# A hand-written order for an attention and phase-mixing kernel, replaced by another order of the same steps

## The chip, the cores and the metric

The kernel runs on one core of one Trainium2 chip. The metric is the device time of the whole program in microseconds (us), lower is better. A profile of one execution stands beside the times; its span runs from the first to the last instruction of the program on the core.

A core has five engines with an instruction stream each: PE (TensorE, matrix products and transposes by an identity matrix; PEld is its weight load, which overlaps), DVE (VectorE), ACT (ScalarE), POOL (GpSimd) and SP (SyncE, which here only issues DMAs). Results of PE land in PSUM, which this kernel uses as 8 banks of 512 float32 per partition.

## The reference

The inputs are `q`, `k`, `v` of 8 batches x 8 heads x 576 positions x 64, and four weight matrices. Two attentions are added: one over positions averaged in groups of four (144 of them), whose result is repeated four times, and one over a band of seven neighbours. Their sum is the input `x` (8 x 576 x 512) of a mixing step with a cosine and a sine of a learned phase.

```python
q_d = q.reshape(B, H, Sd, 4, D).mean(axis=3)          # k_d, v_d alike
out_up = np.repeat(sm_attn(q_d, k_d, v_d), 4, axis=2)
mask = np.abs(pos[:, None] - pos[None, :]) < 4
scores = np.where(mask, scale * q @ k.T, -1e9)
out_local = softmax(scores) @ v
x = (out_up + out_local)                              # heads side by side: 576 x 512
...
theta = x @ w_theta
y = w_tok_r @ (x * cos(theta)) + w_tok_i @ (x * sin(theta))
u = x + y
out = u + np.maximum(u @ w_ch, 0.0)
```

## The kernel before

Everything is unrolled. The work is cut into some 1,190 steps, and a table of words, `ORDER`, says in which order they are emitted. A word is a kind of two letters and a place: the PSUM bank or pair of banks that a PE step writes, the staging slot (0 to f) that a load fills, or the engine (`v` DVE, `a` ACT, `g` POOL) that does a cast, an eviction or a sum. `tp45` is a transpose into banks 4 and 5; `ckv` a cast of a piece of `k` on DVE; `lk8` a load of `k` into slot 8. The indices of a step (batch, piece) don't stand in the word: the n-th word of a kind is the n-th piece of that kind, in a fixed order. `pin()` ties each instruction to the one before it on its engine, so the order of the words is the order in each engine's queue. Between engines the tile framework puts the waits that data, banks and buffers need.

The steps of one batch, with the lines of the profile:

- Loads `lk`, `lq` (L287), `lv`/`lw` (L348) into 16 float32 staging slots; casts to bf16 `ck`, `cq` (L296) and `cv` (L396); transposes `tp` on PE (L303) and their copies `ev` (L316) into `kT`, `qT`. Batch 7 has its `k` and `q` transposed by DMA instead (`dk` L307, then `ev` L313). Batch 0 has its `v` loaded, cast and transposed in another way at the very start: `l1` L366, `c1` L372, `t1` L377, `e1` L380, `x1` L389, `cv` L394.
- Means of four: `kd`, `qd`, one reduction on DVE (L322) or two additions on POOL (L330 and L333 or L336); `pv` (L404, L407) and `vd` (L412, L415) for `v`.
- Coarse attention: scores `sd` (L426), exponential `ed` on ACT (L437), products `nd` (L447, L452), division `xn` on DVE (L457, L458), transpose `xd` (L466) and its copy `xc` (L470).
- Band attention: scores `ps` (L482) in three units of two, two and one chunks, exponential `ex` on ACT (L490), multiplication with the band `mk` on POOL or DVE (L501), products `po` (L511), division `nm` on DVE (L519, L520), transpose `xt` (L533), and `xa` on DVE (L541), which adds the coarse part and gives `xT`, the transposed `x`.
- Phase: `th` (L552) and `tt` (L564) on PE, cosine and sine `cs` (L557, L558) and `ct` (L569, L570) on ACT. `xm` transposes `xT` back on PE (L591) in batches 0 to 5; in 6 and 7 `dx` does it by DMA, four DMAs a batch (L601). `zz` on DVE (L616, or L611 with `dx`) multiplies. The last 64 positions go through `zt` (L573) and `zp`, `zc` (L583, L586) in batches 0 to 3, through a DMA `dz` (L577) in 4 to 7.
- Mixing: `mx`, eight groups of nine matmuls a batch (L632), and `ua` on DVE (L637), which gives `uT`; `up`, `uc` (L646, L649) on PE or `du` by DMA, four a batch (L641), bring `u` back.
- The end: `ch` (L662) on PE, `rl` on DVE (L667), the store `st` (L671). The last 64 positions of two batches together: `ut` (L652), `dt` by DMA (L686), `ht` on PE (L691), `rt` on DVE (L695), stores `ss`, `sr` (L700).

`wm` (L755) is a number of matmuls on a tile of zeros that nobody reads. `wm483` writes bank 4 with eight matmuls of 512 columns and one of 3 x 64. They stand at the start, where PE waits for loads, casts and copies. `te` and `ts` (L761) load the table of the exponential or of the sine into ACT ahead of its use.

A pair of banks is taken as any two banks:

```python
def pair(w):
    a, b = sorted(int(x) for x in w)
    return PS[:, a:b + 1:b - a, :]
```

All DMAs stand in the one queue of SP, in the order of the words. A DMA that has to wait there (for a slot, or for the result that it stores) holds back all DMAs behind it.

Of the kernel before, what the change touches and what calls it, by code (L numbers as in the profile page):

```python
# [58 lines left out]
lq9 x11 tp45 kcg cqa cva cqg x16 cqg lka cvv cvv lqb evv cvv ckg cva lkc kdg cka cqa lqd ckg lke laf wm772 tp23 evv  # L59
wm754 tp67 pv45 tp01 qdv kcg eva vdv la0 kdg lq1 eva cka wm256 ps23 ex ps67 lk2 qdv ps01 mkv wm446 sd45 sd23 ex ed  # L60
po67 ed cav cqg la3 po45 nm nm lk5 nd67 cqa xn mkg nd23 ex xn cag cka tp45 lq6 eva la4 po01 po67 lb8 nm lb9 xd2 wm303
tp45 lb7 cqa lba lqb ckg lbc lbe xcv mkg lbd lbf xt01 caa nm lb1 po23 kdg xa eva lv0 lv2 xt67 tp45 lw cag th0 lv5 cba
cbg lw cbg cqg lw xa xm1 nm th6 xt23 lv6 evv th7 ts cs xa zz tp45 cbg cbg wp0 cs wcv lv3 xm6 cs tt2 xm3 th7 wp1 lw xm0
zz zz lw qdv lk8 wcv eva ct lk4 lq9 cs cbg cbg cbg cbg wp6 wca wp3 wp2 wp4 wp5 wca wp1 wcv wcv wcv wp2 ztg ps67 ps45
qdg wcv te ex wcv ex lq7 kdg lkb lka zz lkc lqe lkd zp1 zcv cvv lqf mx3 cvg cvg cvg mkv ua cvg lq1 mx2 sd01 ps67 lv0
mkv lq2 ex po45 mx3 nm sd67 ua cqg po45 ed lw po01 nm ua nm mx2 ed ua pv67 po45 lq5 mx3 cqg vda nm nd01 ua cka up2
nd67 mkg cka xn ckg ckg lk6 uca xn up3 tp45 uca tp01 xd6 eva ckg xt23 mx7 xcv eva qdg xa xt45 po01 th6 cqg xa lv3 ckg
lv9 tp23 nm ts cs cqa th4 lq7 xm5 xt01 th6 evv cs tp23 xa zz cqa tt4 ua tp01 kdg cs ct cqg evv ztv th5 lw evv lw xm7
zz cs tp23 mx6 xm4 kdg zp5 qdg ua eva zz cvv ps01 cqa ps23 lv8 xm7 kdg zz zcv lk4 te ex lw mx6 mx4 ua mx5 sd01 mkv lvb
lw ua ex po67 mkv cva ps23 qdg lca lcc utg ed lce nm mx4 cvg ex lcd lvf ua lk1 po01 lk2 sd67 lw po23 ckg nm cqa nm mx5  # L70
ckg ed tp01 cvg ua lq5 eva tp67 mx4 lq0 cca ua up5 evv cvg ua ccg ccg pv23 mkg ucv vda lk3 qdv ps01 ps67 ex up4 mx5
ccv nd23 ex ua nd01 uca kdg ch5 po67 xn ps23 ckg cka lv9 mx4 xn tp01 lw ex mkg rl nm lk6 cva ckg xd5 sd23 ua cqg xcv
xt67 lv7 eva mx4 lw lv4 lw cvg xa lv8 lw ed xt01 po23 po67 th5 ua ch4 cqa ts cs xa nm nm th0 po23 lqb xt67 rl up1 cs
nm kdg th5 xm0 xa cs xm4 tp23 xm6 tt7 mkg cvg zz th0 lqc ucv zz st up1 cvg up5 ch4 eva ucv ckg ct ucv ch1 zz po23 cs
sd67 lve lva rl mkv te ed cvg pv45 lqd lk1 ztg cqg ch0 rl rl lk2 ch1 qdg nm lq3 vda tp67 nd45 rl cqa xm0 lqf eva lw zz
xn nd23 zp1 utg lw xn tp67 zca lk5 lq9 kdg mx0 up1 ua po45 lv0 eva ckg lk7 ps23 nm lw po67 nm ckg lv4 uca mx0 tp45 lk6
qdg mx1 ua xd0 ps67 ua lv8 ex eva xca ckg sd23 xt45 xa lw mx1 mkg st cvg ua ed mx0 ex mx1 mkv ua th0 po23 ua xt45 ts
cs xa xt67 mx1 xm0 xa th4 xm5 lqb zz ua tt0 kdg xm1 cvv ckg cvv th6 ch7 cqg cka cqg cs ct nm cs lvc cqg lk1 ztv tp23
eva lw th0 rl zz cs cqg zz tp67 evv cvg xm4 zz st zp5 zca ch1 rl cva tp23 mx0 po67 ua eva ps45 lw nm po23 lv2 te ex
lv5 mx1 pv67 lke cqg st mx0 po45 dt vda nm lk7 mkv st lqd po23 ckg ua ua qdg sd67 ch1 qdg nm nm ht0 cka ed rt lv3 up6  # L80
up7 cvg ucv uca nd45 kdg cqg nd23 mx0 xn lw xn ps67 ss ps45 ex ex xd2 mx3 tp67 xcv up2 cva ua uca tp45 lq6 rl evv up0
cqg lw eva ch1 ua lvf xt67 ps23 ucv sd45 xa cva st ex lw lq9 rl lk4 mx0 sd23 ed xt67 ua ckg xa lva qdg lw mkv kdv xt45
mx1 cvg th0 ua st lvb mx6 ua lw ed mkg tp23 ts cs utg lw mx7 cqg xa ua up6 po01 po45 cvg eva uca pv23 tt7 nm vda lq0
nm th6 xm0 zz nd45 ct cs ch1 lv1 xn cva st tp23 nd67 cva xn up0 th4 xm5 th6 zz sr eva xm7 xm5 ps23 lv8 lvc rl uca cs
po01 ch4 zz lw cs nm zz ztg ch7 te ex dz xd6 ch5 cvg rl lw lqe utg rl mkg po01 ps23 st mx4 lw lkd up7 cqg cka st ex
up2 uca nm ch3 rl xt01 kdg st st cvg xcv cva qdg ckg ua xa mkg uca po45 pv67 mx2 nm mx0 ua lk6 sd45 vda lk2 rl lq7
xt67 cqg ua ps23 xa mx1 lv5 ed po45 ua lq3 nm st mkv cqg dt ex dk9 sd23 xt67 ckg ed mx0 mkg du xa nd45 ch1 ckg ua po23
# [711 lines left out]
```

## Time and profile before

| | |
|---|---|
| three runs | 236.89, 238.10, 238.81 us; median 238.10 |
| span of the profiled execution | 232.1 us |
| outside the span, against the median | 6.0 us |
| PE busy | 220.7 us, 95% of the span |
| DVE, ACT, POOL busy | 191.8, 156.1, 135.5 us |
| DMA, read and written | 33.98 and 9.44 MB of HBM, mean 213 GB/s with the transfers inside SBUF |

The page gives no device time of its own for the profiled execution: its span is 232.1 us, and the 6.0 us to the median are what lies around a span. Matmuls are pipelined, and a row of PE counts each from its start to its modelled end, so that a PE that is busy is not a PE at its peak: what a group of matmuls costs the queue is read from how far apart many of them in a row start.

### The profile page before, as it was taken

Reading aid. Unit: us, or ns where it says so; the run is one execution under the profiler, and the core shown is the slowest. Engines: PE = TensorE matmul, PEld = TensorE weight load, DVE = VectorE, ACT = ScalarE, POOL = GpSimd, SP = SyncE. Lnnn points to the kernel's source line nnn. Section 1 sums busy time; section 2 is a strip of 40 time slices with the busy share of each in tenths; the row PEclk is TensorE's granted clock in tenths of the full one; section 3 lists DMA queues with packets and bytes.
Section 4 is the critical chain, followed back from the end, with each engine's and each line's share of the span. In section 5 each row is a group of like instructions: output and inputs, shape, how many; then the busy total and the mean of one; then the engine's idle time right before and its main releaser. Section 6 shows DMA issues by size and latency. Waiting matters only on the chain.

```text
span 232.1 us, 9462 instructions
## 1 busy us (share of the span) xinstructions
PE 220.7 (95%) x3986; PEld 153.2 (66%) x3986; DVE 191.8 (83%) x365; ACT 156.1 (67%) x241; POOL 135.5 (58%) x179
## 2 busy tenths in 40 slices
PE   7998899999998999999999999999999998999991
PEld 2665678777776765776768766676676563767750
DVE  6699999989997988868997997799889967567572
ACT  3359999799877989867976979857766591620000
POOL 7468989869999656897472837767386510000000
PEclk9999999999999999999999999999999999999998
DMA  6999989999999899989606895899957766556676
GB/s 204 382 392 390 298 134 252 365 263 193 264 263 195 224 290 208 203 209 210 174 3 178 226 234 147 293 249 173 153 122 189 144 138 100 154 126 182 138 235 217
DMA packets 76795, 49.41 MB, mean 213 GB/s; under 512 B 61136, under 2 KB 61392, under 8 KB 76752
## 3 DMA queue, kind: packets, MB, share of 16 engines
q1 hardware_dynamic: 76752, 48.81, 84.6%
q8 instruction: 31, 0.51, 1.1%
q14 instruction: 12, 0.10, 0.2%
HBM read 33.98 MB, written 9.44 MB: 187 GB/s over the span
## 4 chain that ended last, share of the span: by engine, by line
PE 72%; DVE 12%; DMA 5%; SPq 3%; issue 3%; ACT 2%; DVEq 0%
PE PS L632 24%; PE PS L662 10%; PE PS L552 9%; PE PS L303 5%; PE PS L755 4%; PE PS L511 3%; DVE xT L541 3%; DMA out_dram<-osb 2%; DVE pm L501 2%; PE PS L591 2%; PE PS L482 2%; DMA st<-xT 2%; SPq L641 2%; PE PS L533 2%; DVE uT L637 2%
## 5 line engine op out<-in xcount | busy, mean ns | idle before, releaser
L632 PE MATMUL PS<-WT,z 128*128 128x288 bf16 x576 | 77.9, 286 | 1.7 <-issue 1.7
L632 PEld LDWEIGHTS <-z 128*128 128x128 bf16 x576 | 53.8, 98 | 17.5 <-issue 2.8
L637 DVE TENSOR_TENSOR uT<-PS,xT 128x288 bf16<-128x288 f32 x64 | 28.1, 450 | 11.4 <-PE PS L632 11.1
L552 PE MATMUL PS<-wth,xT 128*128 128x512 bf16 x128 | 32.3, 380 | 0.7 <-DVE xT L541 0.7
L557 ACT ACTIVATE cs<-PS,pihc 128x512 bf16<-128x512 f32 x32 | 22.3, 696 | 15.1 <-PE PS L552 9.9
L662 PE MATMUL PS<-wch,uT 128*128 128x512 bf16 (+1 forms) x132 | 30.6, 373 | 0.0
L520 DVE TENSOR_TENSOR tmp<-PS,rl 128x512 bf16<-128x512 f32 x40 | 27.7, 692 | 1.4
L541 DVE TENSOR_TENSOR xT<-PS,xdT 128x928 bf16<-128x928 f32 (+1 forms) x24 | 22.7, 952 | 3.4 <-PE PS L533 3.1
L490 ACT ACTIVATE pm<-PS 128x1024 bf16<-128x1024 f32 (+1 forms) x24 | 20.4, 877 | 7.0 <-PE PS L482 2.7
L501 POOL TENSOR_TENSOR pm<-pm,band 128x1024 bf16<-128x1024 bf16 (+1 forms) x13 | 22.2, 1709 | 2.9 <-ACT pm L490 2.9
L667 DVE SCALAR_TENSOR_TENSOR osb<-PS,ur 128x512 f32<-128x512 f32 (+1 forms) x33 | 21.8, 669 | 2.4 <-PE PS L662 1.6
L330 POOL TENSOR_TENSOR two<-kT 128x580 f32<-128x580 bf16 x15 | 17.5, 1163 | 6.1 <-ACT kT L316 5.2
L296 POOL CAST q_tm<-st 128x576 bf16<-128x576 f32 x22 | 14.4, 664 | 10.8 <-DMA st<-in_q_dram 10.8
L662 PEld LDWEIGHTS <-uT 128*128 128x128 bf16 x132 | 12.2, 98 | 12.2 <-issue 0.3
L558 ACT ACTIVATE cs<-PS 128x512 bf16<-128x512 f32 x32 | 19.4, 605 | 0.0
L330 POOL TENSOR_TENSOR two<-qT 128x576 f32<-128x576 bf16 x11 | 12.8, 1167 | 10.5 <-ACT qT L316 7.1
L552 PEld LDWEIGHTS <-xT 128*128 128x128 bf16 x128 | 11.2, 98 | 10.7 <-issue 1.3
L616 DVE TENSOR_TENSOR z<-PS,cs 128x1024 bf16<-128x1024 bf16 x24 | 16.2, 685 | 1.9 <-PE PS L591 0.9
L437 ACT ACTIVATE pd<-PS 128x864 bf16<-128x864 f32 x16 | 14.1, 889 | 5.2 <-PE PS L426 5.2
L761 ACT ACT_TABLE_LOAD x13 | 16.7, 1283 | 0.2
L296 POOL CAST k_tm<-st 128x576 bf16<-128x576 f32 x21 | 14.4, 695 | 1.4 <-DMA st<-in_k_dram 1.4
L396 POOL CAST v_w<-st 128x512 bf16<-128x512 f32 x21 | 13.3, 653 | 1.3 <-DMA st<-in_v_dram 1.2
(119 smaller groups left out, 419.3 us busy)
## 6 DMA issues: line engine op xcount, KB each, us to landing
st<-in_q_dram SPq DMA_DIRECT2D x32, 288.0 KB, 6.3
st<-in_k_dram SPq DMA_DIRECT2D x32, 288.0 KB, 6.0
st<-in_v_dram SPq DMA_DIRECT2D x70, 128.0 KB, 4.7
out_dram<-osb SPq DMA_DIRECT2D x31, 256.0 KB, 2.9
out_dram<-osb SPq DMA_DIRECT2D x10, 128.0 KB, 2.4
st<-in_v_dram SPq DMA_DIRECT2D x4, 288.0 KB, 3.7
st<-in_moe_w_tok_r_dram SPq DMA_DIRECT2D x4, 288.0 KB, 6.2
st<-in_moe_w_tok_i_dram SPq DMA_DIRECT2D x4, 288.0 KB, 7.2
```

Source lines behind the costliest of these rows:

```text
L296: COPY[w](out=to[:, r, :], in_=of[:, r, :])
L330: nc.gpsimd.tensor_tensor(out=t, in0=src[:, :, 0:2], in1=src[:, :, 2:4], op=ALU.add)
L490: nc.scalar.activation(out=pm[(3 * b + u) % NPM][:, :, 0:n].rearrange("p e c j w -> p e (c j w)"), in_=at.pop(("ps", b, u))[:, :, 0:4 * W ...
L501: EW[w].tensor_tensor(out=t, in0=t, in1=m, op=ALU.mult)
L520: nc.vector.tensor_tensor(out=tmp[(NCH * b + c) % NTMP].rearrange("p g (j d) -> p g j d", d=D), in0=ps[:, :, :, 0:D], in1=r.unsqueeze(3).t ...
L541: nc.vector.tensor_tensor(out=xT[b % 2][:, :, lo:lo + cnt].rearrange("p e (m j) -> p e m j", j=4), in0=at.pop(("xt", b, u))[:, :, 0:cnt].r ...
L552: nc.tensor.matmul(out=ps, lhsT=xT[b % 2][:, dc, P * c:P * c + P], rhs=wth[:, dc, :], start=(dc == 0), stop=(dc == 3))
L557: nc.scalar.activation(out=t[:, 0, :], in_=ps, func=AF.Sin, bias=pihc, scale=1.0)
L632: nc.tensor.matmul(out=ps, lhsT=z[b % 2][:, j, P * dc:P * dc + P], rhs=WT[:, j, cols], start=(j == 0), stop=(j == 8))
L637: nc.vector.tensor_tensor(out=uT[b % 2][:, dc, cols], in0=at.pop(("mx", b, i)), in1=xT[b % 2][:, dc, cols], op=ALU.add)
L662: nc.tensor.matmul(out=ps[:, cols], lhsT=uT[b % 2][:, dc, P * c:P * c + P], rhs=wch[:, dc, cols], start=(dc == 0), stop=(dc == 3))
L667: nc.vector.scalar_tensor_tensor(out=o[:, cols], in0=at["ch", b, c][:, cols], scalar=0.0, in1=ur[b % 2][:, c, cols], op0=ALU.max, op1=ALU.add)
```

## The change

Only the table `ORDER` changes: all its 39 lines are new. The steps, their indices, tiles, buffers and shapes stay. In the new table

- the steps stand in another order, on every engine and in SP's queue;
- banks, slots and engines are other ones. The pairs of banks were 01, 23, 45 and 67 (150 results, and 8 `pv`, whose two banks were such pairs too); now they are 01, 23, 45, 67 and also 12, 34 and 56 (20 of 150). `pv` has two results of one bank each and now also takes 07, 57 and 04;
- `wm` has 22 matmuls of 512 columns and 25 x 64 columns; before 40 and 31 x 64. They still stand at the start only;
- casts and evictions have moved between engines. Counts before and now: `ck` on DVE 1 and 11, on POOL 21 and 12, on ACT 10 and 9; `cq` on DVE 0 and 4, on ACT 10 and 7; `mk` on DVE 11 and 6, on POOL 13 and 18; `qd` on DVE 5 and 1, on POOL 11 and 15; `ev` on DVE 9 and 7; `te` and `ts` together 13 and 15.

```diff
 ORDER = """
-l10 l11 l12 c1v c1a c1g k0 l13 kcv wm061 t101 c1g lq4 e1v wm256 t123 lk5 lk6 kca e1v wm483 x12 x13 lk7 ckv lq8 x10 cka
...
+l10 l11 c1v c1v l12 c1g l13 c1g wm785 t101 wm712 t123 lk4 ckv lk5 ckg wm736 tp45 lk6 ckg lq7 e1a e1v x13 x12 x10 lq8
...
 """
```

(`k0` is a word without an instruction.)

Three places follow. First the queue of DVE at the start of the program, from behind the first casts of `v` to the first multiplication with the band (`z_103` holds `v` of batch 0 here, `xT_102` its transpose, `k_tm` and `q_tm` the cast `k` and `q`, `st` the staging slots). Before:

```order
L296 CAST k_tm_74<-st 128x8x64
L296 CAST k_tm_74<-st 128x64
L394 CAST v_w_70<-PS 128x8x64 x2
L316 COPY kT_62<-PS 128x2x576
L394 CAST v_w_70<-PS 128x8x64
L316 COPY qT_64<-PS 128x1152
L322 TENSOR_REDUCE qd_68<-qT_64 128x288
L412 CAST vd_72<-PS 128x8x64
L415 CAST vd_72<-PS 32x4x64 x2
L322 TENSOR_REDUCE qd_68<-qT_64 128x288
L501 TENSOR_TENSOR pm_83<-pm_83,band 128x1024
```

Now, without the rows between `q_tm_78` and `k_tm_76` (two more casts of `q`, `vd` and `kd`):

```order
L296 CAST k_tm_74<-st 128x8x64
L296 CAST k_tm_74<-st 128x64
L380 COPY xT_102<-PS 128x1152
L231 COPY pu_132<-full_136 64x32 x2
L231 COPY pu_133<-full_137 64x32 x2
L231 COPY band<-full_135 64x64 x2
L394 CAST v_w_70<-PS 128x8x64
L296 CAST k_tm_75<-st 128x8x64
L296 CAST k_tm_75<-st 128x64
L394 CAST v_w_70<-PS 128x8x64
L296 CAST q_tm_78<-st 128x8x64
L296 CAST q_tm_78<-st 128x64
```

The copies of `kT` and `qT` (`ev`) and the sums of `qd` have left this stretch of DVE's queue for ACT and POOL; casts of `k` and `q` and small constants have come in, and the first cast of `k` now stands ahead of the copy of `xT_102`.

Second, the queue of DVE where batch 7's `xT` and batch 6's `z` are made (`xT_102` is batch 7 and `z_103` batch 6 here). Before:

```order
L470 COPY xdT_100<-PS 128x576
L541 TENSOR_TENSOR xT_102<-PS,xdT_100 128x4x232
L611 TENSOR_TENSOR z_103<-st,cs_105 128x1024
L541 TENSOR_TENSOR xT_102<-PS,xdT_100 128x4x232
L611 TENSOR_TENSOR z_103<-st,cs_106 128x1024
L541 TENSOR_TENSOR xT_102<-PS,xdT_100 128x4x112
L611 TENSOR_TENSOR z_103<-st,cs_107 128x1024
L611 TENSOR_TENSOR z_103<-st,cs_108 128x1024
```

Now, a little further down, where `uT_111` is batch 6 and `z_104` batch 7:

```order
L637 TENSOR_TENSOR uT_111<-PS,xT_101 128x288
L695 SCALAR_TENSOR_TENSOR osb_119<-PS,utr 128x512
L611 TENSOR_TENSOR z_104<-st,cs_105 128x1024
L611 TENSOR_TENSOR z_104<-st,cs_106 128x1024
L611 TENSOR_TENSOR z_104<-st,cs_107 128x1024
L637 TENSOR_TENSOR uT_111<-PS,xT_101 128x288
```

All three `xa` of batch 7 now stand ahead of the four `zz` of batch 6; and three `zz` of batch 7 stand between the first and the second `ua` of batch 6.

Third, the queue of SP that feeds those `zz`: `st_126<-xT0_101` are the `dx` of batch 6, `st_126<-xT1_102` those of batch 7. Now:

```order
L601 DMA_TRANSPOSE st_126<-xT0_101 128x4x128
L671 DMA out_0_dram<-osb0_118 128x512
L671 DMA out_0_dram<-osb1_119 128x512
L671 DMA out_0_dram<-osb3_121 128x512
L671 DMA out_0_dram<-osb4_122 128x512
L700 DMA out_0_dram<-osb2_120 64x512
L641 DMA_TRANSPOSE ur1_114<-uT1_112 128x4x128 x3
L601 DMA_TRANSPOSE st_126<-xT0_101 128x4x128 x3
L577 DMA_TRANSPOSE z0_103<-zT_110 128x4x128
L641 DMA_TRANSPOSE ur1_114<-uT1_112 128x4x128
L671 DMA out_0_dram<-osb0_118 128x512
L601 DMA_TRANSPOSE st_126<-xT1_102 128x4x128 x3
```

Behind these come `dt`, `dz`, one store and the fourth `dx` of batch 7. Before, two `dx` of batch 6 stood first, with two stores, three `du`, two `dx`, a store, `dz`, `dt`, a `du`, two `dx`, two stores and two `dx` behind them: 14 transposes and 5 stores from the first `dx` to the last, now 15 and 7.

More of the change, by code (lines that the diff above doesn't have):

```diff
@@ L57 @@
 ORDER = """
-l10 l11 l12 c1v c1a c1g k0 l13 kcv wm061 t101 c1g lq4 e1v wm256 t123 lk5 lk6 kca e1v wm483 x12 x13 lk7 ckv lq8 x10 cka
[L59 to L87, printed above, removed]
@@ new lines @@
+eva kcv kcv kcg kcv cvv x11 cva lk9 lqa lqb x17 ckv lk0 lk2 lk3 cva cvv cva cqg cqg cqv wm623 tp23 eva tp45 eva pv07
+cqv wm621 tp12 vdv eva kdg qdg qdg kdv wm652 ps01 ps23 la4 cag ckv lb5 cka ckv ex ex cbg lb6 cbg mkv wm716 tp67 la7
+lk8 mkg sd01 sd45 ed lq9 lqa ed po23 nm po01 caa lqb cqg eva nd23 cqa cqg nm nd45 ps01 la1 lac ex mkg xn cka xn po67
+po23 cag xd4 kdg lb2 lv0 lb3 lb4 tp01 xca nm nm xt67 lv5 tp45 xa xt23 cbg cbg lq7 eva xa cbg caa ts po01 nm xm6 lb6
+lbd th7 th3 lb9 xt01 cbg cbg cbg lbb evv cs th2 xa xm7 zz cqg wp4 lq8 cs cs zz xm5 tt3 zz th0 ct lva wp7 wp6 cs wcv
@@ L97 @@
+mx1 mx4 ua ztg dz st rt mx5 mx7 dx ss zz zz cs zz ua du mx1 cs zz mx3 mx0 ua ua rl rl ua mx2 mx7 mx6 ua ua mx1 mx3 ua
+ua mx2 mx0 ua ua ua ua sr mx1 ch3 st ua du du utv du ua ua du du st ch0 st rl st du ch1 ch2 ch3 ch7 ch6 ch5 du uta rl
+st rl rl st dt rl st st st rl st rl rm st su rl st ht7 rt sr ss k0
 """
```

39 lines of the change are left out of this document (30 added, 9 removed).

## The prediction

> **What bounds the kernel now.** I read the page's span and busy times first, then the busy time of each engine in a few stretches, then the chain of waits at its end. The page:
>
> ```profile
> span 232.1 us, 9462 instructions
> PE 220.7 (95%) x3986; PEld 153.2 (66%) x3986; DVE 191.8 (83%) x365; ACT 156.1 (67%) x241; POOL 135.5 (58%) x179
> ```
>
> PE is busy for all but 11.4 us. The stretches show where those are; columns: from and to, length, then busy us (and instructions) of PE, PEld, DVE, ACT and POOL, the granted clock, the DMA share and GB/s:
>
> ```profile
> 6.00:18.00 12.00, 12.00 (x136) 7.32 (x133) 9.82 (x12) 5.41 (x8) 7.04 (x13) 1.00 1.04 390
> 18.00:30.00 12.00, 10.26 (x333) 7.34 (x334) 11.44 (x23) 11.95 (x18) 10.90 (x14) 1.00 1.05 325
> 40.00:180.00 140.00, 137.42 (x2810) 99.15 (x2802) 122.33 (x223) 112.76 (x171) 100.82 (x118) 1.00 0.91 210
> 196.00:227.10 31.10, 31.04 (x224) 20.62 (x222) 21.09 (x43) 5.23 (x10) 0.00 (x0) 1.00 0.64 170
> ```
>
> From 40 to 180 us PE idles for 2.6 of 140 us, DVE for 17.7; from 196 us to PE's end, 0.06 of 31.1. So the body is PE's own queue, with DVE next. From 18 to 30 us DVE (11.44 of 12) and ACT (11.95) are full and PE is not: there PE waits. From 6 to 18 us PE looks full, but much of that is `wm`:
>
> ```profile
> L755 PE MATMUL PS<-warm 128*128 128x512 bf16 (+5 forms) x48 | 11.6, 380 | 0.0
> ```
>
> These 11.6 us stand where PE would wait. What an order can win is then 11.6 us of fill, 1.7 us between 18 and 30 us, and some 3 us behind. The useful work of PE doesn't change: the same groups stand in both tables. Its pace at the end:
>
> ```profile
> 204.93 14.33 PE PS L632 x117
> 219.26 6.92 PE PS L662 x36
> ```
>
> 117 matmuls are 13 `mx` groups, 1.10 us each; the 36 of `ch` are 7 whole groups and one in halves, 0.87 us each.
>
> **The start.** The first `th` needs `xa`, and `xa` comes at the end of a long queue on DVE. The timeline at its two ends (start, length, engine, line, what; in brackets the idle time ahead and what ended it):
>
> ```profile
> 7.08 0.67 POOL L372 CAST z<-st 128x576 bf16<-128x576 f32 x1 [0.18 <-DMA st<-in_v_dram]
> 8.51 1.36 DVE L380 COPY xT<-PS 128x1152 bf16<-128x1152 bf16 x1 [0.56 <-PE PS L377]
> 9.24 0.67 ACT L296 CAST k_tm<-st 128x576 bf16<-128x576 f32 x1 [3.92 <-DMA st<-in_k_dram]
> 27.75 1.11 DVE L541 TENSOR_TENSOR xT<-PS,xdT 128x928 bf16<-128x928 f32 x1
> 27.89 1.04 PE L552 MATMUL PS<-wth,xT 128*128 128x512 bf16 x4
> ```
>
> From 9.87 us (the copy's end) to 28.86 us (the second `xa`'s) DVE hardly waits, so what leaves this stretch of its queue brings `th` forward. The prices, by form:
>
> ```profile
> L296 DVE CAST k_tm<-st 128x512 bf16<-128x512 f32 x1 | 0.4, 427 | 0.0
> L372 DVE CAST z<-st 128x64 bf16<-128x64 f32 x1 | 0.3, 285 | 0.0
> L231 DVE COPY pu<-full 64x32 bf16<-64x32 bf16 x2 | 0.4, 207 | 0.0
> L322 DVE TENSOR_REDUCE qd<-qT 128x288 bf16<-128x1152 bf16 x5 | 6.7, 1346 | 0.1
> L316 DVE COPY kT<-PS 128x1152 bf16<-128x1152 bf16 x6 | 8.1, 1352 | 0.3 <-PE PS L303 0.3
> L394 DVE CAST v_w<-PS 128x512 bf16<-128x512 f32 x3 | 2.0, 685 | 0.5 <-PE PS L389 0.5
> L243 DVE CAST wth<-st 128x512 bf16<-128x512 f32 x1 | 0.4, 420 | 0.0
> ```
>
> In come five casts of `k` and `q` (0.43 + 0.29 each, 3.6 us), six small copies (1.2) and one sum of `kd` (taken as 1.35, as `qd`): 6.1 us. Out go two `ev` (2.7), two `qd` (2.7), one cast of `v_w` (0.7), one of `wth` (0.4), the copy `xc` to ACT (taken as 0.4) and the first cast of `k`, which now lies ahead of the copy (0.7): 7.6 us. That is 1.5 us less. The stretch starts later, though: the copy now stands behind the first cast of `k`. The fourth load of `v` landed at 7.08 us, the sixth load (`k`) at 9.24; the first `k` is now the fifth, so at 8.2, cast by 8.9, and the copy ends at 10.2 rather than 9.87. Together -1.2 us. Behind this comes POOL's first `mk`, which now has two sums of `qd` and three weight casts ahead of it, and ends about when it did (23 us). The ends: nothing, if the first `k` lands at 9.24 as it did; and -5.0, if PE's waits shrink as their fill does: 40 x 512 + 31 x 64 = 22,464 columns took 11.6 us, 22 x 512 + 25 x 64 = 12,864 would take 6.6. I take -1.2, because DVE's queue is the row that was full.
>
> **The body.** The casts that moved, and what they cost beside POOL's work:
>
> ```profile
> L396 DVE CAST v_w<-st x5: 410/793/1266, 38.0 to 173.6; 128x512 bf16<-128x512 f32 x5
> 40.14 0.72 DVE L501 TENSOR_TENSOR pm<-pm,band 128x1024 bf16<-128x1024 bf16 x1
> 177.35 2.19 DVE L501 TENSOR_TENSOR pm<-pm,band 128x1024 bf16<-128x1024 bf16 x1
> 176.87 3.69 POOL L501 TENSOR_TENSOR pm<-pm,band 128x1024 bf16<-128x1024 bf16 x2 [1.93 <-ACT pm L490]
> L501 DVE TENSOR_TENSOR pm<-pm,band 128x1024 bf16<-128x1024 bf16 x9 | 11.0, 1217 | 0.0
> L501 POOL TENSOR_TENSOR pm<-pm,band 128x1024 bf16<-128x1024 bf16 x7 | 14.9, 2123 | 2.9 <-ACT pm L490 2.9
> L330 POOL TENSOR_TENSOR two<-qT 128x576 f32<-128x576 bf16 x11 | 12.8, 1167 | 10.5 <-ACT qT L316 7.1 <-ACT qT L313 1.8 <-PE PS L533 1.4
> L336 POOL TENSOR_TENSOR qd<-two 128x288 bf16<-128x288 f32 x11 | 7.6, 695 | 0.9
> L296 POOL CAST k_tm<-st 128x576 bf16<-128x576 f32 x21 | 14.4, 695 | 1.4 <-DMA st<-in_k_dram 1.4
> ```
>
> Over the whole program DVE gives up four `qd` (5.4 us), four long `mk` and a short one (5.5), two `ev` and the copy of batch 0 (4.1), and takes 14 casts (14 x 0.71 = 9.9); the small moves add some 2: about -3 us. POOL takes four long `mk` (8.5), four `qd` (4 x 1.86 = 7.4) and gives up nine casts of `k` (6.3): with the small moves +13 of 135.5. ACT loads a table twice more and drops casts: about even. DVE's saving lies at the start; ahead of the first two `mx` groups it has 4.7 us less to do at these means, so behind them some 1.7 us more. It had 17.7 us to spare from 40 to 180 us, and PE paid 2.6 us. I take +0.8 us for tighter turns of banks and DVE's later work; the ends are -2.6 (all of PE's idle time goes) and +4.5 (below).
>
> The row of 2.19 us: the same multiplication took 0.72 us at 40.14, and 2.19 where POOL did one of its own from 176.87 on. DVE's ended 0.5 us after POOL's first. So DVE waited for POOL. The Trainium skill, "SBUF — State Buffer", section "Who interferes with whom", says that DVE and GpSimd share a pair of ports as an exclusive lock: a DVE instruction with two SBUF inputs, or a copy or cast in a 2-port mode, waits for a whole GpSimd instruction that came first, or makes it wait. The trace agrees (2.19 against 0.72). By this rule each of the 14 casts on DVE would wait up to one POOL multiplication, and the move of `mk` to POOL would lengthen what they wait for; that speaks against the change.
>
> **The end.** Before, a `zz` of batch 6 that waited for a DMA stood ahead of `xa` of batch 7, and PE waited for that `xa`:
>
> ```profile
> 195.82 1.02 PE L552 MATMUL PS<-wth,xT 128*128 128x512 bf16 x4 [0.66 <-DVE xT L541]
> 205.58 0.68 DVE L611 TENSOR_TENSOR z<-st,cs 128x1024 bf16<-128x1024 bf16 x1
> 206.18 0.45 DVE L637 TENSOR_TENSOR uT<-PS,xT 128x288 bf16<-128x288 f32 x1
> ```
>
> This 0.66 us goes, since `xa` is ahead now. What is late next is `zz` of batch 7: three of them stand ahead of the second `ua` of batch 6, whose bank (1) the sixth `mx` of batch 6 needs. A `zz` needs all four `dx` of its batch, and the fourth is the last of 15 transposes and 7 stores on SP. SP's prices:
>
> ```profile
> 180.10 2.53 SPq L601 DMA_TRANSPOSE st<-xT  x2
> 183.11 1.58 SPq L671 DMA_DIRECT2D out_dram<-osb  x2
> 184.78 3.84 SPq L641 DMA_TRANSPOSE ur<-uT  x3
> 201.58 2.52 SPq L601 DMA_TRANSPOSE st<-xT  x2
> ```
>
> A transpose holds SP for 1.27 us, a store for up to 0.79; 15 and 7 are at least 19 and up to 24.6 us; take 23. From the last issue's end (204.10) to the `zz` behind it (205.58) it was 1.5 us, then three `zz` at 0.6 and a `ua` of 0.45: 26.8 us after the first `dx` of batch 6 the bank is free. PE has, from that `dx`'s place in the table to the `mx`, 8 `mx` groups (8.8), 15 of `th`, `ch` and `ht` (13.0) and small groups (estimated 3): 24.8 us. So the `dx` has to issue 2 us before PE passes its place. Its data (`xa` of batch 6) are there some five PE groups ahead, and two `du` are the only transposes just before it, so I take it that it does, and price the end at -0.6; the ends are -0.7 and +3.5, where the `dx` comes 1.5 us behind its place instead.
>
> **The sum.** -1.2 + 0.8 - 0.6 = -1.0 us on the span of 232.1, so 231.1; with the 6.0 us around the span that separate it from the median of 238.1, **237.1 us**. The runs before lie within 0.8% of each other, so a difference of 1% (2.4 us) is about what can be told from none.
>
> **The rivals.**
>
> *The fill tells the truth* (faster): PE's waits at the start shrink by 5.0 us. 238.1 - 5.0 + 0.8 - 0.6 = 233.3. For it: the fill is cut at every place, and ACT, also full from 18 to 30 us, loses two casts there. Against: DVE's queue shrinks by only 1.2.
>
> *SP is late at the end* (slower): the `dx` of batch 6 issue at their place or later, the sixth `mx` of batch 6 waits for `ua` behind three `zz`. It decides once SP is more than 2 us later than I take it; at 1.5 us behind its place it costs 3.5: 237.1 + 3.5 = 240.6. For it: SP's row is nearly unbroken from 184 to 204 us, and the new stretch has three entries more. Against: the `xa` come earlier.
>
> *DVE waits for POOL* (slower): the casts at 0.8 us rather than 0.4 (the median of five against the least) and up to 1.3 add 14 x 0.4 = 5.6 to 12 us to DVE; six `mk` fewer take back 6 x 0.5 = 3.0. At +4.5 on PE's path, in place of the 0.8: 240.8. It decides once DVE's idle share in the body (17.7 of 140) falls under a tenth. This is what the Trainium skill's rule above would make of it.
>
> That the table isn't followed can't be, since each queue is pinned to it; that other pairs of banks cost or save something by themselves, no row shows.
>
> **The numbers.** The forecast has 0.38, and its own range is 235 to 239.3: of it 0.12 are below 235.7 (faster by over 1%), 0.25 within, 0.01 above 240.5. The fill: 0.25, all faster. SP late: 0.14, of which 0.10 slower, 0.04 within. DVE behind POOL: 0.17, 0.13 and 0.04. Gains and losses that cancel in other places: 0.06, within. Faster 0.37, same 0.39, slower 0.24. The range of 232.6 to 241.6 takes in all four times and leaves out what lies beyond the fill's and the two slow cases' own prices.
>
> **What would show it.** Right: the first `th` near 26.7 us, `wm` near 6.6 us, PE idle 2 to 4 us from 40 to 180, no wait of `th` for `xa` in the last 40 us, and `zz` of batch 7 done before PE has passed five `mx` of batch 6. The fill rival: `th` before 24 us. SP late: PE idle 2 us or more ahead of an `mx` of batch 6, ended by `uT` or by a DMA. DVE behind POOL: casts L296 on DVE at 0.8 us or more in their larger half, DVE busy over 126 us from 40 to 180. Wrong altogether: long waits of PE in the body for casts or transposes of `k` and `q`, or a start later than 27.9.

## The result, and the profile after

The changed kernel takes 252.97 us (median of 4 runs, 249.90 to 255.72), the kernel before on the same chip 237.50 us. The ratio is 1.064, with a 95% interval of 1.052 to 1.076: 15.5 us slower. The forecast was 237.1 us, with a range of 232.6 to 241.6.

Each run's time is 1.7 us above its span. So the profiled execution of before (span 232.1) took 233.8 us and was one of its fastest; the one of after took 255.7 and was its slowest. The two profiles are 21.9 us apart, the medians 15.5: sizes read from the two profiles are upper ones, and what a change is worth is taken from the ratios.

The head of the page after:

```profile
span 254.0 us, 9417 instructions
PE 223.3 (88%) x3967; PEld 154.1 (61%) x3967; DVE 200.8 (79%) x388; ACT 156.2 (62%) x240; POOL 149.4 (59%) x180
```

DVE is busy for 9 us more than before (191.8), not 3 us less; POOL for 13.9 us more, as forecast. The stretches of after, with the columns of the prediction:

```profile
18.00:30.00 12.00, 8.54 (x298) 6.93 (x296) 10.88 (x20) 9.69 (x14) 9.86 (x11) 0.86 0.96 287
40.00:180.00 140.00, 125.25 (x2523) 89.14 (x2510) 117.14 (x217) 107.99 (x168) 104.72 (x113) 0.99 0.90 199
205.00:249.00 44.00, 41.12 (x344) 25.77 (x340) 27.35 (x49) 8.79 (x17) 2.08 (x2) 0.96 0.66 135
```

From 40 to 180 us PE now idles for 14.75 us, where it idled for 2.6. DVE and ACT are less busy in that stretch than before (122.33 and 112.76): no engine is full, and PE waits nevertheless (the DMA share, 0.90, is what it was, 0.91). For what, the longest of PE's waits from 18 us on say (who waited, for whom; us in total, times, the longest one; "issue" is a stop for which the profile names nobody):

```profile
PE PS L426 <- POOL kd L333: 3.7, 2, 2.5
PE PS L632 <- DVE osb L695: 2.6, 1, 2.6
PE PS L511 <- DVE pm L501: 1.7, 1, 1.7
PE PS L564 <- issue: 1.6, 1, 1.6
PE PS L662 <- DVE z L616: 1.5, 1, 1.5
PE PS L511 <- DVE osb L667: 1.4, 1, 1.4
PE PS L447 <- DVE tmp L520: 1.0, 1, 1.0
PE PS L407 <- POOL v_w L396: 0.9, 1, 0.9
```

They are many and of many kinds: sums of `kd`, casts of `v`, a multiplication with the band, an addition at the end.

To see where they add up, the trace gives PE's lag. The work in front of each group of matmuls is summed at the price of groups that follow each other without a wait (1.10 us for `mx`, 0.86 for `th`, `ch` and `ht`, down to 0.13 for the smallest `ps`; 195.3 us in all). From the time at which the group's result is taken up (the start of the copy, sum or function that reads it), that sum is subtracted, and the least of each 10 us of work stands here:

| lag (us) at PE's work of | 20 | 60 | 100 | 150 | 180 |
|---|---|---|---|---|---|
| before | 18.8 | 23.3 | 25.8 | 29.1 | 31.7 |
| after | 21.6 | 35.4 | 44.3 | 48.3 | 53.4 |

So the start costs 2.8 us, the body some 15 to 16 (most of it before half of the work is done), the end 2.5 to 4. The last two can't be parted more finely: the lag of before rises from 29.1 to 31.7 just there, so it matters where the body is cut off.

### The profile page after: what moved, and what is told of

It reads as the page before. It is cut to its first block, busy times and chain, and to the rows that moved or that the text cites. A ratio compares the mean times of both kernels' runs of the same rounds, so it can differ in the third digit from the quotient of the medians.

```text
span 254.0 us, 9417 instructions
## 1 busy us (share of the span) xinstructions
PE 223.3 (88%) x3967; PEld 154.1 (61%) x3967; DVE 200.8 (79%) x388; ACT 156.2 (62%) x240; POOL 149.4 (59%) x180
## 4 chain that ended last, share of the span: by engine, by line
PE 39%; DVE 20%; DMA 16%; POOL 8%; SPq 6%; issue 6%; ACT 3%; DVEq 0%; POOLq 0%; ACTq 0%
PE PS L632 17%; DMA st<-in_v_dram 7%; DMA st<-in_k_dram 5%; PE PS L662 4%; PE PS L552 4%; DMA out_dram<-osb 3%; DVE k_tm L296 3%; POOL two L330 2%; DVE z L616 2%; PE PS L511 2%; DVE uT L637 2%; SPq L348 2%; PE PS L533 2%; DVE osb L667 2%; DVE v_w L396 2%
## 5 line engine op out<-in xcount | busy, mean ns | idle before, releaser
L632 PE MATMUL PS<-WT,z 128*128 128x288 bf16 x576 | 79.5, 293 | 3.4 <-DVE osb L695 2.6
L632 PEld LDWEIGHTS <-z 128*128 128x128 bf16 x576 | 55.4, 100 | 19.5 <-issue 3.9
L501 POOL TENSOR_TENSOR pm<-pm,band 128x1024 bf16<-128x1024 bf16 (+1 forms) x18 | 32.1, 1791 | 6.1 <-ACT pm L490 6.1
L557 ACT ACTIVATE cs<-PS,pihc 128x512 bf16<-128x512 f32 x32 | 22.1, 691 | 14.1 <-PE PS L552 14.0
L437 ACT ACTIVATE pd<-PS 128x864 bf16<-128x864 f32 x16 | 13.9, 892 | 12.6 <-PE PS L426 12.5
L296 POOL CAST q_tm<-st 128x576 bf16<-128x576 f32 x21 | 13.9, 674 | 12.5 <-PE PS L303 8.2
L330 POOL TENSOR_TENSOR two<-qT 128x576 f32<-128x576 bf16 x15 | 17.6, 1172 | 5.4 <-ACT qT L316 4.3
L552 PEld LDWEIGHTS <-xT 128*128 128x128 bf16 x128 | 11.8, 99 | 11.9 <-issue 0.9
L573 POOL TENSOR_TENSOR zT<-xT,cst 128x512 bf16<-128x512 bf16 x6 | 7.5, 1246 | 18.5 <-ACT cst L570 12.5
L396 POOL CAST v_w<-st 128x512 bf16<-128x512 f32 x20 | 12.4, 633 | 8.9 <-DMA st<-in_v_dram 8.8
```

The costliest lines, as they stand in the source:

```text
L296: COPY[w](out=to[:, r, :], in_=of[:, r, :])
L330: nc.gpsimd.tensor_tensor(out=t, in0=src[:, :, 0:2], in1=src[:, :, 2:4], op=ALU.add)
L501: EW[w].tensor_tensor(out=t, in0=t, in1=m, op=ALU.mult)
L552: nc.tensor.matmul(out=ps, lhsT=xT[b % 2][:, dc, P * c:P * c + P], rhs=wth[:, dc, :], start=(dc == 0), stop=(dc == 3))
L557: nc.scalar.activation(out=t[:, 0, :], in_=ps, func=AF.Sin, bias=pihc, scale=1.0)
L632: nc.tensor.matmul(out=ps, lhsT=z[b % 2][:, j, P * dc:P * dc + P], rhs=WT[:, j, cols], start=(j == 0), stop=(j == 8))
```

## The experiments

### Order or engines

Two kernels cross the two tables: the order of the one with the engine letters of the other. For example

```diff
 # the changed order, engines of before
-l11 c1v c1v l12 c1g l13
+l11 c1v c1a l12 c1g l13
...
 # the order of before, engines of the changed table
-cqg lka cvv cvv lqb evv
+cqg lka cva cva lqb eva
```

> The changed table in its new order, with the engine of each cast, eviction and sum set back to what the same piece had before (120 words of the table differ, among them 20 casts of k, 14 of q, 21 of v, 13 copies ev, 9 mk, 6 qd). Theory 'engines' (the 15 us come from casts on DVE that wait beside POOL, and from POOL's longer list): most of it returns, 238 to 243 us. Theory 'loads' (they come from v of batch 1 and later halves of v landing behind k and q of later batches, with POOL's queue held behind the cast that waits): little returns, 249 to 254 us, since SP's order stays. Theory 'margins' (the order as a whole leaves PE less ahead of what it waits for): 247 us or more, perhaps above 253, since engines that were chosen for the new order are taken away.

> The table of before in its order, with the engine of each cast, eviction and sum as the changed table has it for the same piece (120 words differ). 'Engines': 245 to 253 us. 'Loads': 238 to 242 us, since no load moves. 'Margins': anything from 238 to 246, and less than half of the 15 us.

Measured: 264.19 us, ratio 1.123 (1.114 to 1.132), and 251.67 us, 1.065 (1.055 to 1.075). Each mixture is about as slow as the changed kernel, or slower. "Engines" and "loads" fail on the first: it should have returned most or nothing, and it lost 11 us more. "Loads" fails on the second too, where no load moves and 14 us are lost. "Engines" is right on the second alone (245 to 253), "margins" on the first alone. The engine of a cast and its place in the order fit together, and neither by itself explains the result.

### The loads

In the first pair most loads of `q`, `k` and `v` are left out:

```diff
             t = at["s", n, b, hh] = stg[int(w, 36)]
+            if b >= 2 and (n, b, hh) not in ((0, 2, 0), (0, 4, 2), (1, 4, 3)):
+                return
...
+        if b >= 2 and (b, c) != (2, 4):
+            return
         lo = W0[2 * c + g]
```

> The changed kernel without the loads of q, k and v of batches 2 to 7 (all but k(2,0), k(4,2), q(4,3) and a piece of v of batch 2, so that no slot is read before it was filled once); the casts take what a slot still holds, all other work stays. 'Loads': the distance to the same kernel made from before shrinks from 15 to under 7 us, and PE's lag grows in the body by at most 13 us instead of 27. 'Engines' and 'margins': the distance stays at 10 us or more.

> The kernel before without the same loads, to stand beside the changed kernel without them. 'Loads': before was not held by its loads, so 233 to 238 us. If before, too, is held by its loads, it falls below 233.

Measured: 245.60 us, ratio 1.043 (1.037 to 1.048), and 233.48 us, 0.989 (0.985 to 0.993). The distance is 12.1 us instead of 15.5: loads are a part, 3 us more in the changed kernel than in the other, but not the bulk. The changed kernel's lag still grows by 17.3 us in the body (22.1 us at 20 us of work, 39.4 at 170; with all loads it was 27.3), more than the 13 that "loads" allowed.

The second pair keeps all loads and puts them, on the same places of the table, in the order in which their casts stand; slots are chosen to fit:

```diff
 # the changed table
-lk6 ckg lq7 e1a e1v x13 x12 x10 lq8
+lk6 ckg lk7 e1a e1v x13 x12 x10 lq8
...
-ps01 ps23 la4 cag ckv lb5 cka ckv
+ps01 ps23 lkf cag ckv lb0 cka ckv
```

> The changed kernel with the words of its loads (k, q, v, weights) put on the same places in the order in which their casts stand in the table, with staging slots chosen to fit; nothing else moves. The changed table has 331 pairs of loads that stand against the order of their casts, before has 120. Theory 'loads': 4 to 8 us off, 245 to 249, since leaving most loads out took 7.4 us off; the gain lies between 30 and 70 us of the span. If the queues' fullness and not the order of loads was what leaving them out removed: 251 to 254.

> The kernel before with its loads put on the same places in the order in which their casts stand in the table. It has 120 pairs against that order, the changed one had 331. Leaving most loads out took 4.2 us off it. 'Order of loads': 235 to 238, a small gain or none. If a changed order of loads always costs in an order made for another: 238 to 242.

Measured: 247.53 us, 1.043 (1.034 to 1.051), so 5 us off, all that leaving loads out had given by the ratio; and 235.14 us, 0.995 (0.990 to 1.000), in the old table, a gain within what can be told from none. So some 4 of the 5 us belong to the changed order of loads. One place is shown by POOL's timeline. In the changed kernel:

```profile
39.09 1.35 POOL L396 CAST v_w<-st 128x512 bf16<-128x512 f32 x2
41.73 0.62 POOL L396 CAST v_w<-st 128x512 bf16<-128x512 f32 x1 [1.29 <-DMA st<-in_v_dram]
42.30 1.59 POOL L330 TENSOR_TENSOR two<-kT 128x580 f32<-128x580 bf16 x1
43.97 1.00 POOL L333 TENSOR_TENSOR kd<-two 128x290 bf16<-128x290 f32 x1
44.92 0.66 POOL L296 CAST q_tm<-st 128x576 bf16<-128x576 f32 x1
47.07 0.61 POOL L396 CAST v_w<-st 128x512 bf16<-128x512 f32 x1 [1.49 <-DMA st<-in_v_dram]
48.37 0.61 POOL L396 CAST v_w<-st 128x512 bf16<-128x512 f32 x1 [0.69 <-DMA st<-in_v_dram]
```

and with loads by need:

```profile
39.90 1.72 POOL L396 CAST v_w<-st 128x512 bf16<-128x512 f32 x3
41.58 1.15 POOL L330 TENSOR_TENSOR two<-kT 128x580 f32<-128x580 bf16 x1
42.81 0.67 POOL L333 TENSOR_TENSOR kd<-two 128x290 bf16<-128x290 f32 x1
43.42 1.13 POOL L296 CAST q_tm<-st 128x576 bf16<-128x576 f32 x1
44.50 1.63 POOL L396 CAST v_w<-st 128x512 bf16<-128x512 f32 x2
```

A cast of `v` that waits for its load holds POOL's queue, and the sum of `kd` for which PE waits stands behind it. In POOL's waits of the changed kernel this is the row

```profile
POOL v_w L396 <- DMA st<-in_v_dram: 8.8, 5, 3.2
```

and with loads by need no such row is left. The casts of batch 1's `v` that ended at 49.0 end at 46.1.

### The fill and the clock

In the profiles the changed kernel's granted clock falls to a half three times before PE's end, that of before not once. Stretches of after with the clock in the third column from the end, and one of the kernel before with less fill:

```profile
18.00:24.60 6.60, 3.47 (x135) 2.32 (x133) 6.03 (x10) 6.29 (x9) 5.82 (x6) 1.00 0.99 320
24.60:28.00 3.40, 3.06 (x78) 2.86 (x78) 2.88 (x8) 1.47 (x3) 2.04 (x4) 0.50 0.86 203
86.00:89.40 3.40, 0.89 (x72) 0.79 (x68) 0.43 (x3) 0.96 (x2) 3.24 (x5) 1.00 0.80 213
89.40:92.80 3.40, 3.40 (x16) 1.75 (x13) 2.55 (x3) 2.31 (x4) 3.40 (x4) 0.51 1.07 284
226.00:229.40 3.40, 3.40 (x17) 2.14 (x15) 3.40 (x8) 0.00 (x0) 0.00 (x0) 0.50 0.33 70
23.00:29.70 6.70, 5.59 (x115) 5.04 (x106) 5.67 (x14) 3.02 (x5) 3.08 (x4) 0.50 1.09 286
```

Ahead of the first two, PE had been busy for 3.47 of 6.60 us and for 0.89 of 3.40. The Trainium skill, "TensorE: Matmul & The Clock Gate", section "What's actually happening", says that TensorE's clock is at a half after a window of about 3.4 us in which it was idle. The stretches here agree in their length, 3.4 us or twice that, though PE was busy for part of the time ahead of them.

```diff
 # the changed table: 26 matmuls of fill more, at four waits
-ed lq9 lqa ed po23 nm
+ed lq9 lqa ed wm280 po23 nm
...
 # the table of before: fill of 22 instead of 40
-lq4 e1v wm256 t123 lk5 lk6 kca e1v wm483 x12 x13
+lq4 e1v wm236 t123 lk5 lk6 kca e1v wm443 x12 x13
```

> The changed kernel with 26 more matmuls of 512 columns on the tile of zeros, at four of PE's long waits: 8 ahead of the first po, 5 ahead of the first nd, 9 ahead of the first xt of batch 2, 4 ahead of the first th of batch 2 (every fourth matmul of fill that the change had taken away stands at the start; there it was 40, then 22, now 35). Theory 'clock' (behind PE's idle stretches the granted clock falls to a half for 3.4 us, which costs up to 1.7 us each time; the changed kernel's profile has this from 24.6 and from 89.4 us, before has none until PE's end): both half-clock stretches go, 2 to 4 us off the median of 253. Rival (the fill is a cost, or PE's waits hide the slow clock): 253 to 256.

> The kernel before with its fill cut from 40 to 22 matmuls of 512 columns, at the same eight places. This is the prediction's rival 'the fill tells the truth' taken alone. If fill is only a cover for waits: 237 to 239, same as before. If waits shrink with it: 233 to 235. 'Clock': a half-clock stretch comes up between 10 and 30 us, 239 to 242.

Measured: 255.18 us, 1.074 (1.063 to 1.084), and 238.06 us, 1.005 (0.999 to 1.011). More fill took the half-clock stretch at 24.6 us away and gained nothing, though its profile has one of 3.4 us at 60.6 that was not there before, and the one near 90 us stayed. Less fill brought one in the old kernel (the last row above) and cost nothing that can be measured. So at the start the time at a slow clock lay where PE would have waited anyway, within a per cent, and my theory that the clock made the 15 us falls. So does the prediction's rival of the fill: with the same fill as the changed kernel, the old one isn't faster.

### The store at the end

The tail of after, in the timeline of DVE, PE and SP:

```profile
220.08 0.46 DVE L637 TENSOR_TENSOR uT<-PS,xT 128x288 bf16<-128x288 f32 x1 [3.09 <-ACT cs L557]
224.03 0.69 DVE L695 SCALAR_TENSOR_TENSOR osb<-PS,utr 128x512 f32<-128x512 f32 x1 [3.49 <-DMA out_dram<-osb]
224.77 5.51 PE L632 MATMUL PS<-WT,z 128*128 128x288 bf16 x30 [2.59 <-DVE osb L695]
213.36 0.53 SPq L671 DMA_DIRECT2D out_dram<-osb  x1
213.99 3.83 SPq L601 DMA_TRANSPOSE st<-xT  x3
217.92 1.21 SPq L686 DMA_TRANSPOSE utr<-ut  x1
219.24 2.19 SPq L577 DMA_TRANSPOSE z<-zT  x1
221.53 0.54 SPq L671 DMA_DIRECT2D out_dram<-osb  x1
```

`rt` waits for a free `osb` buffer, that buffer for its store, and the store stands behind five transposes in SP's queue (five, not the eight that the expectation counts), the last of which holds it for 2.19 us. PE waits for `rt`, because the bank of the fourth `mx` of batch 6 is free only behind it. One word was moved, first in the changed kernel, then in one with loads by need and casts on ACT (next part):

```diff
-cs cs du st th0 th3 dx9 dx zz dxb zz zz cs dt rl rl mx7 mx1 mx4 ua ztg dz st rt mx5
+cs cs du st st th0 th3 dx9 dx zz dxb zz zz cs dt rl rl mx7 mx1 mx4 ua ztg dz rt mx5
```

> The changed kernel with one word moved: the store of piece (4,3), which the profile shows as the last thing that the third rt waited for (3.49 us on DVE, and 2.6 us on PE behind it), stands directly behind the store of (4,2), ahead of six transposes and two dz in SP's queue. Theory 'SP late by a store': PE's stall ahead of the fourth mx of batch 6 goes, and with it the half-clock stretch at 226 us: 2.5 to 4.5 us off, 248.5 to 250.5. If zz of batch 7 and their transposes are next (the prediction's own rival, through dx): 0 to 1.5 us off.

> The changed kernel with loads by need, its casts of k and q on ACT instead of DVE (241.3 us), and the store of (4,3) ahead of the six transposes and two dz. Moving that store alone in the changed kernel took 2.4 us of lag out of the profile's tail but nothing off the median. If the tail's wait is real and was hidden by what the body varies: 239 to 240 us. If something else is next there: 240.8 to 241.8.

Measured: 253.50 us, 1.068 (1.058 to 1.078), against 1.064 without the move; and 240.57 us, 1.019 (1.010 to 1.029), against 1.021. In the profile of the first, PE's wait for `rt` falls from 2.6 to 0.7 us and the lag at the end by 2.4 us, but no gain shows in the times. The wait and its cause are shown; a price of it in the times isn't, and is within a per cent.

### The casts on DVE

First the engines of the changed table in the old order, one group at a time:

```diff
 # casts of k and q (34 words)
-xn cag cka tp45 lq6 eva
+xn cag ckv tp45 lq6 eva
...
 # mk, qd, kd (17 words)
-pv45 tp01 qdv kcg eva vdv la0 kdg
+pv45 tp01 qdg kcg eva vdv la0 kdv
...
 # everything else (69 words)
-cqg lka cvv cvv lqb evv
+cqg lka cva cva lqb eva
```

> The table of before, with only the engines of the casts of k and q as the changed table has them for the same piece (34 words: 15 casts on DVE instead of 1, 33 on POOL instead of 43, 16 on ACT instead of 20). All the changed table's engines together, in the order of before, cost 14 us. Theory 'lock' (a cast on DVE takes 1.1 to 1.3 us beside POOL's work instead of the 0.72 that I took, and who waits for DVE pays): 5 to 9 of the 14 us, 243 to 247. Theory 'each engine choice fits its own order': 2 to 5 us from each of three groups.

> The table of before, with only the engines of mk, qd and kd as the changed table has them (17 words: mk 9, qd 6, kd 2; POOL gets 5 mk and 4 qd more). POOL's multiplications hold the lock longer and POOL's list grows by 13 us. 'Lock' and 'POOL is late': 3 to 6 us, 241 to 244. 'Each choice': 2 to 5 us.

> The table of before, with the engines of everything else as the changed table has them (69 words: cv 21, ev 13, uc 9, the casts of weights, xc, wc, zc, zt, ut and the casts of batch 0's v). 'Lock': 0 to 2 us, 238 to 240, since DVE gets little more here. 'Each choice': 3 to 6 us.

Measured: 247.87 us, 1.042 (1.028 to 1.055); 241.00 us, 1.012 (1.003 to 1.020); 244.85 us, 1.034 (1.027 to 1.042). The casts of `k` and `q` are the largest by the median, but not told from the rest by the intervals, and the three don't add up: 8.8% one by one, 6.5% together. Both theories are half right: "lock" expected the casts to cost most, but next to nothing of the rest; "each choice" expected the rest to cost, but less of the casts and of the rest than they did.

The rows of these casts on DVE, in the changed kernel, say why they cost (least, median and most ns; each cast is two instructions, 512 and 64 columns):

```profile
L296 DVE CAST k_tm<-st x22: 184/634/1861, 8.1 to 139.0; 128x512 bf16<-128x512 f32 x11, 128x64 bf16<-128x64 f32 x11
L296 DVE CAST q_tm<-st x8: 180/416/1251, 14.5 to 97.8; 128x512 bf16<-128x512 f32 x4, 128x64 bf16<-128x64 f32 x4
59.77 0.52 DVE L296 CAST k_tm<-st 128x512 bf16<-128x512 f32 x2
100.68 3.42 POOL L501 TENSOR_TENSOR pm<-pm,band 128x1024 bf16<-128x1024 bf16 x2
101.23 2.92 DVE L296 CAST k_tm<-st 128x512 bf16<-128x512 f32 x2
```

At 59.77 POOL did nothing, and the pair took 0.52 us. At 101.23 POOL was at its two multiplications, and the same pair took 2.92 us, as one instruction waited for the first of them to end (at about 102.8) and the other for the second (104.1). In all the 30 instructions took 18.9 us. Three edits tell waiting from being queued: the casts on ACT; each cast as one instruction, still on DVE; and the six such casts of the old kernel on ACT.

```diff
 # on ACT
-t123 lk4 ckv lk5 ckg wm736
+t123 lk4 cka lk5 ckg wm736
...
 # one instruction
-            for r in ((slice(0, WR - 1), slice(WR - 1, WR)) if w == "v" else (slice(0, WR),)):
+            for r in (slice(0, WR),):
                 COPY[w](out=to[:, r, :], in_=of[:, r, :])
...
 # before
-zp1 zcv cvv lqf mx3
+zp1 zcv cva lqf mx3
```

> The changed kernel with its loads in the order of need (247.5 us), and besides its 15 casts of k and q on DVE put on ACT. 'Lock': DVE's busy time falls by the 22 us that those casts took there, 3 to 6 us come off, 241.5 to 244.5. 'Each choice' (the order is left without the engine that it was made for): 247 to 250.

> The changed kernel with loads by need (247.5 us), the casts of k and q left on DVE, but each as one instruction of 576 columns instead of 512 and 64. Theory 'lock' (each DVE instruction waits for the POOL instruction that runs; the casts of 64 columns took 0.18 us alone and 0.65 or 1.14 us beside POOL): 15 waits fewer, DVE's casts take 14 to 18 us in all instead of 21.8, and 1 to 4 us come off, 243.5 to 246.5. If what costs is only that DVE has 15 pieces more in its queue: 246.5 to 248.5.

> The changed kernel as it is, table untouched, with the casts of k and q on DVE as one instruction of 576 columns. With the loads by need this took 6.6 us off (247.5 to 240.9), and the row of these casts went from 0.18 to 1.86 us to an even 0.74 to 0.75. Theory 'two instructions that wait for POOL, independent of the loads': 245.5 to 248 us. If the loads hide it when they stand in the changed order: 249.5 to 253.

> The kernel before with the six casts that it has on DVE from SBUF in the body (one of k, five of v; 4.7 us in all, up to 1.27 us each) on ACT. 'Lock': 0.5 to 2 us off, 235.5 to 237.5. 'Each choice fits its own order': 238 to 241.

Measured, on the changed kernel with loads by need (1.043, 1.034 to 1.051): on ACT 241.28 us, 1.021 (1.016 to 1.026); as one instruction on DVE 240.93 us, 1.021 (1.013 to 1.029). On the changed kernel as it is, one instruction: 248.10 us, 1.060 (1.053 to 1.067). In the old kernel, 237.74 us, 1.005 (1.000 to 1.009): no gain, where "lock" expected one; what its few casts on DVE cost doesn't show. On the changed kernel with loads by need both edits gained some 5 us by the ratios: as much as "lock" expected of the casts on ACT (3 to 6), and more than it expected of the casts as one instruction (1 to 4).

The rows of the casts as one instruction, from the kernel with loads by need, and one of them beside POOL's multiplications:

```profile
L296 DVE CAST k_tm<-st x11: 736/743/754, 8.5 to 127.2; 128x576 bf16<-128x576 f32 x11
L296 DVE CAST q_tm<-st x4: 742/744/745, 13.7 to 87.0; 128x576 bf16<-128x576 f32 x4
89.31 1.15 POOL L573 TENSOR_TENSOR zT<-xT,cst 128x512 bf16<-128x512 bf16 x1
90.10 0.74 DVE L296 CAST k_tm<-st 128x576 bf16<-128x576 f32 x1
90.42 3.24 POOL L501 TENSOR_TENSOR pm<-pm,band 128x1024 bf16<-128x1024 bf16 x2
```

It is 0.2 us slower alone, and never waits: 0.736 to 0.754 us each, whatever POOL does (at 90.10 POOL was at one multiplication until 90.46, and then at the next two); 11.2 us in all instead of the 21.8 that the cut casts took in this kernel. That brings as much as taking the 15 casts off DVE altogether. So, once the loads are in order, it was the waiting that cost, not the place in DVE's queue.

The lag shows where (us at PE's work; "both" is loads by need and one cast):

| lag (us) at PE's work of | 20 | 60 | 100 | 150 | 180 |
|---|---|---|---|---|---|
| after | 21.6 | 35.4 | 44.3 | 48.3 | 53.4 |
| loads by need | 22.7 | 28.5 | 40.8 | 43.7 | 46.3 |
| one cast | 19.0 | 32.2 | 37.7 | 40.7 | 43.2 |
| both | 19.0 | 25.6 | 32.1 | 35.7 | 38.2 |
| before | 18.8 | 23.3 | 25.8 | 29.1 | 31.7 |

In these profiles one cast takes out the whole loss of the start, and the two gains stand beside each other. The ratios say less for the one cast alone: 1.060 and 1.064 overlap, where the medians are 4.9 us apart; between 1 and 5 us, the runs don't settle it.

### What is left

The last run gives the kernel with both repairs the engines of `mk`, `qd` and `kd` that before had:

```diff
-eva kdg qdg qdg kdv wm652
+eva kdg qdv qdv kdg wm652
```

> The changed kernel with loads by need and casts of one instruction (240.9 us), and the engines of mk, qd and kd as before (17 words), whose change alone cost 2.7 us in the old table. If that price belongs to POOL's longer list: 237.5 to 239.5. If each table's engines fit its own order: 240.5 to 243.5.

Measured: 245.37 us, 1.045 (1.036 to 1.054), where 1.021 stood. POOL's longer list is not what is left; in the new order those engines are the right ones. The 2% that remain, some 4 to 5 us, I could not put down to one thing; their cause stays open. No kernel that does the whole work is faster than before by more than its interval.

## Why the prediction was wrong

- **What bounds.** That PE's queue sets the pace and DVE comes next was read rightly for before. Wrong was what I drew from it: that a DVE with 17.7 us to spare of 140 takes a few us without harm. After, no engine is full from 40 to 180 us, and PE idles for 14.75 of it. A share of busy time doesn't say how early each piece is done.
- **The 6.0 us around the span.** They are 1.7: the profiled execution took 233.8 us, not 238.1. The forecast's base (238.1) stands all the same.
- **The start, -1.2 us: measured +2.8.** Right were the fill (6.8 us, forecast 6.6) and the list of what comes in and goes out. The end of the copy (10.18 us, forecast 10.2) was met in part by luck: the first cast of `k`, behind which it was to stand, was done by 8.6 rather than 8.9, and then the copy waited 0.20 us for PE. The term that failed is the price of what comes in:

```profile
8.82 1.36 DVE L380 COPY xT<-PS 128x1152 bf16<-128x1152 bf16 x1 [0.20 <-PE PS L377]
10.88 1.16 DVE L231 COPY band<-full 64x64 bf16<-64x64 bf16 x2
12.80 1.19 DVE L296 CAST k_tm<-st 128x512 bf16<-128x512 f32 x2
14.51 2.26 DVE L296 CAST q_tm<-st 128x512 bf16<-128x512 f32 x4
19.44 2.62 DVE L296 CAST k_tm<-st 128x512 bf16<-128x512 f32 x4
29.27 2.15 DVE L541 TENSOR_TENSOR xT<-PS,xdT 128x928 bf16<-128x928 f32 x2
30.68 1.89 PE L552 MATMUL PS<-wth,xT 128*128 128x512 bf16 x8
```

The five casts took 6.07 us for 3.6, two of the six copies 1.16 for 0.41. The second `xa` ends at 31.42 us instead of 28.86, and `th` starts at 30.68; forecast was 26.7. POOL's first `mk` ended at 25.1, not "about when it did (23 us)". With casts of one instruction, `th` starts at 27.33 and the start's loss is gone.

- **The body, +0.8 us: measured some +15 to 16 in the profiles.** Two steps failed. "Takes 14 casts (14 x 0.71 = 9.9)": the 15 that stand there took 18.9, which is 9 of the 12 us by which DVE's busy time missed its forecast (9 us more rather than 3 less). And the order of the loads has no term in the sum at all, though the change says that SP's queue is new: 331 pairs of loads stand against the order of their casts, 120 did. The order of the loads was worth some 5 us (1.064 to 1.043), the waiting casts another 5 once the loads were in order (1.043 to 1.021). What the body loses beyond that has no term either. The mixtures show that the engines and the order must fit each other (either one alone costs as much as the whole change or more); that this is what the rest of the body's loss is made of, no run shows.
- **The end, -0.6 us: measured +2.5 to +4 in the profiles, not told from zero in the times.** That the 0.66 us of PE's wait for `xa` go was right: no such wait is left. SP's lateness came, but through a store that `rt` needs, ahead of the fourth `mx` of batch 6, not through `dx` and `zz` ahead of the sixth. SP's term was too small as well: in the profile the 15 transposes and 7 stores took 27.1 us (196.27 to 223.33, with their waits), where 23 was taken and 24.6 was the most.
- **The rivals.** "The fill tells the truth" is refuted by the old kernel with a fill of 22. "SP is late at the end" had the effect (2.6 us of idle PE, priced at 3.5) at another place; with the ends that the prediction itself gives, -0.6 and +3.5, its time would have been 241.2, not 240.6. "DVE waits for POOL" had the mechanism. Its sign came in part: 8 of the 30 instructions took 0.8 us or more, and 9 of the 15 casts over 1.0 us in their two parts. Its price of 4.5 us is near what the waits cost once the loads were in order (some 5); as a time for the whole change 240.8 was far too low, since the loads and the rest are not in it. The point from which it should decide was wrong: DVE's busy time from 40 to 180 us fell to 117.14, well under 126. It isn't DVE's sum that pays, but each piece that comes late. I had quoted the rule of the Trainium skill that names the lock; the row of 2.19 us stood beside it; and I took the price of the casts from a row (0.43) in which POOL was idle.
- **"Wrong altogether"** was named by its signs, "long waits of PE in the body for casts or transposes of `k` and `q`, or a start later than 27.9": the second came. Of the first, PE waited for casts of `q` and `k` only at the start (1.1 and 0.9 us); in the body it waited for sums of `k` in their place.

## What to carry to other kernels

Price an operation that moves to an engine by what stands beside it there, not by its fastest row: here a cast on DVE beside a busy GpSimd lasted until GpSimd's instruction was done (up to 1.86 us for 0.41), and a cast in two instructions could pay that twice. When a table of loads changes while the DMA is nearly full (a share of 0.9 here), compare the order of the loads with the order in which their data are used, and ask what stands behind the instruction that waits for the last of them. And where order and engines have been chosen together, price them together: either half alone may lose as much as both, or more.

## What the runs showed of the hardware

- The same cast of 576 columns takes 0.52 us as 512 + 64 where POOL is idle and up to 2.92 us beside it, and 0.74 us as one instruction, always. The Trainium skill, "SBUF — State Buffer", section "Who interferes with whom", has a copy or cast on DVE take the ports that it shares with GpSimd only in a 2-port mode; and "VectorE: DVE Perf Modes", section "Mode 2×_2P — use both read ports for one tensor", wants the outermost dimension that isn't one to be even, or odd and equal in source and destination. The source here is 576 columns in a row and the destination 9 x 64 in steps, or 8 x 64 and 64 when it is cut in two. The runs agree: 0.41 us for 512 columns and 0.18 for 64 make 0.5 ns a column and 0.15 us besides (an estimate from these two), so the uncut cast at 0.74 us takes 1.0 ns a column, half the rate, and it doesn't wait.
- Half-clock stretches cost nothing measurable at the start, where PE was waiting anyway (1.005, 0.999 to 1.011, with one of 6.8 us).
- PE stopped twice for some 2 us ahead of an `xt` for which the profile names no releaser; the row is of the kernel with loads by need and casts on ACT. The kernels with few loads have no row of this line over 0.5 us. The traces hold a hint: over all 20 profiles PE has, from 10 us on, 38 stops of more than 0.5 us without a releaser, and each of them ends 1.3 to 1.8 us after the end of one of the 31 transfers of 16 KB in the queue that the page calls `q8 instruction`. So PE may have waited for its own instructions, which came late while loads filled the DMA; no run was made to test this, and the cause stays open.

```profile
PE PS L533 <- issue: 4.0, 2, 2.2
```
